# Backward of two normalisations: the mean and dot-product scalars scaled in place, and an affine part moved to ScalarE

## The chip, the cores and the metric

The kernel runs on one core of a Trainium2 chip. The metric is the device time of one launch in microseconds (us). A core has a matrix engine (TensorE, PE in the profile; its weight loads are PEld), a vector engine (VectorE, DVE), a scalar engine (ScalarE, ACT), a general engine (GpSimd, POOL) and an engine that issues transfers (SyncE, SP). Each works through its own list of instructions; an instruction can wait for one of another engine or for a transfer.

## The reference

The kernel computes the output and all gradients of a small two-layer model. A layer is a convolution part (A) and a feed-forward part (B), each on a normalised input and each added to its input:

```python
x = A_q
x = x + _A_ref(_layernorm(x, axis=-1), A_k, A_v, A_shift_k, A_ssm_k, A_ssm_D)
x = x + _B_ref(_layernorm(x, axis=-1), B_w1, B_w2)
x = x + _A_ref(_layernorm(x, axis=-1), A_k, A_v, A_shift_k, A_ssm_k, A_ssm_D)
x = x + _B_ref(_layernorm(x, axis=-1), B_w1, B_w2)
```

The sequence has 2048 rows of D = 448 features; B goes through F = 1792 hidden features with silu. A multiplies its normalised input n by a Y that is the same in both layers. For the backward pass of a normalisation with output n and incoming gradient u (already multiplied by 1/std), the gradient of its input is

    u - mean(u) - n * mean(u * n)

with both means over the 448 features, and the gradient that goes past the normalisation is added. This is what the change touches. It is computed 64 times, for 16 tiles of 128 rows, two layers and two normalisations in each.

## The kernel before

**Stages.** A prefix makes Y with a Fourier transform on TensorE (to about 110 us). Then come layer 1 forward, layer 2 forward woven with layer 2 backward (to about 395 us), layer 1 backward (to about 513 us), and a suffix with the weight gradients and the backward Fourier transform. The rows are worked in 4 chunks of 4 tiles (128 rows each). `L` is 1 for layer 2 and 0 for layer 1.

**One backward chunk.** `ga` multiplies the incoming gradient with w2 in seven pairs of 512-column products `ps_g`. Each pair lies in one of the two PSUM buffers of tag "mm". ScalarE copies it to `ghp` (L690), which frees the buffer for TensorE, and VectorE multiplies it with the silu slope into `ghT` (L698). The slopes are made in place by ScalarE (L614), in layer 1 from `dTl`, which is loaded back from HBM. Then `gn` runs for each of the four tiles: TensorE sums `ps_n` (14 products, L741), ScalarE moves it to `u0`, multiplied by 1/std, with its row sum as accumulator output into `cp` (L743), and `ln_bwd` on VectorE gives the gradient `g1` (in `X` for layer 2, in `G` for layer 1). VectorE makes `gYb` (L753, or L756 and L757) and `u1` with its row sum (L759), and a second `ln_bwd` follows for normalisation A. `u0` and `u1` share one tag with two buffers, so L743 of the next tile but one waits until VectorE is through with an earlier one.

**`ln_bwd`.** L716 multiplies u by n and accumulates the row sum into the second column of `cp`; L718 scales both columns by -1/448 into `cc`. In layer 2 and for the first normalisation of layer 1, two scalar_tensor_tensor follow (L727 adds n times the second scalar, L728 the first scalar and the residual). The second normalisation of layer 1 passes `s`: ScalarE then makes `v`, n times the second scalar plus the first (L721), and VectorE adds u, residual and v with two tensor_tensor (L722, L723).

**What else is in the queues.** In layer 2 the chunk's backward is woven with the next chunk's forward: `ps_h` products share the "mm" buffers, ScalarE makes `aT` (silu, L629) and VectorE `dT` (L113). After the last `aT` ScalarE loads a table and makes eight slopes before the next `na` (normalisation, L273) or `ghp`. In layer 1 products of a weight gradient (`ps_d`, L905) are put between the backward ones.

**Order.** A scheduler with costs for every instruction sets the order on each engine. A balancer (`k.bal`) that adds up estimated loads picks the engine of some copies and normalisations. Engines keep the order that the scheduler gave them.

Of the kernel before, what the change touches and what calls it, by code (L numbers as in the profile page):

```python
# [10 lines left out]
FP32 = mybir.dt.float32  # L11
BF16 = mybir.dt.bfloat16
ACT = mybir.ActivationFunctionType
ALU = mybir.AluOpType
# [3 lines left out]
P = 128  # L18
S = 2048
D = 448  # L20
# [227 lines left out]
def _pm(ap2d):  # L248
    return ap2d.rearrange("(p j) d -> p j d", j=J)
# [230 lines left out]
class Main:  # L480
# [231 lines left out]
    def ln_bwd(self, u0, n_t, cp, g_res, G_out, s=None):  # L712

        nc = self.nc
        junk = self.ch.tile([P, D], BF16, name="lb_junk", tag="lb_junk", bufs=1)
        nc.vector.scalar_tensor_tensor(out=junk[:], in0=u0, scalar=1.0, in1=n_t, op0=ALU.mult, op1=ALU.mult, accum_out=cp[:, 1:2])  # L716
        cc = self.ch.tile([P, 2], FP32, name="lb_cc", tag="lb_cc", bufs=2)
        nc.vector.tensor_scalar(out=cc[:], in0=cp, scalar1=-1.0 / D, scalar2=None, op0=ALU.mult)  # L718
        if s is not None:
            v = self.ch.tile([P, D], BF16, name="lb_v", tag="a_t1")  # L720
            nc.scalar.activation(v[:], n_t, ACT.Identity, bias=cc[:, 0:1], scale=cc[:, 1:2])  # L721
            nc.vector.tensor_tensor(out=s, in0=u0, in1=g_res, op=ALU.add)  # L722
            nc.vector.tensor_tensor(out=G_out, in0=s, in1=v[:], op=ALU.add)  # L723
            self.k.bal.add("dve", 1.5)
            self.k.bal.add("act", 0.64)
            return
        nc.vector.scalar_tensor_tensor(out=u0, in0=n_t, scalar=cc[:, 1:2], in1=u0, op0=ALU.mult, op1=ALU.add)  # L727
        nc.vector.scalar_tensor_tensor(out=G_out, in0=u0, scalar=cc[:, 0:1], in1=g_res, op0=ALU.add, op1=ALU.add)  # L728
        self.k.bal.add("dve", 2.0)

    def gn(self, c, L, ghT, nb, gres, na, hook=None):
        nc, k = self.nc, self.k
        sl = slice(4 * c, 4 * c + 4)
        si = 2 * L
        cp = self.ch.tile([P, 8, 2], FP32, name="cp", tag="cp", bufs=1)
        G = k.X[:, sl, :] if L == 1 else self.ch.tile([P, 4, D], BF16, name="G0", tag="gb", bufs=2)
        for tl in range(4):
            t = 4 * c + tl
            pn = k.psum.tile([P, 512], FP32, name="ps_n", tag="tr" if L == 1 and tl % 2 else "po", bufs=2)
            for ft in range(NF):  # L740
                mm = nc.tensor.matmul(pn[:, :D], lhsT=ghT[ft // 7][:, ft % 7, tl * P:(tl + 1) * P], rhs=self.w1T[:, ft, :], start=(ft == 0), stop=(ft == NF - 1))  # L741
            u0 = self.ch.tile([P, D], FP32, name="lb_u0", tag="lb_u0", bufs=2)
            last_u = nc.scalar.activation(u0[:], pn[:, :D], ACT.Identity, scale=k.rstd[2 * L + 1][:, t:t + 1], accum_out=cp[:, tl, 0:1])  # L743
            k.bal.add("act", 0.75)
            k.pe_engine = mm.ins.engine
            if L == 0:
                self.fill(2 if c < 3 else 12)
            if hook:
                hook(tl, mm.ins, last_u.ins)
            g1 = G[:, tl, :]  # L750
            self.ln_bwd(u0[:], nb[:, tl, :], cp[:, tl, :], gres(tl), g1)
            if L == 1:
                nc.vector.tensor_tensor(out=k.gYb[:, t, :], in0=g1, in1=na[:, tl, :], op=ALU.mult)  # L753
            else:
                gy = self.ch.tile([P, D], BF16, name="gy", tag="lb_junk", bufs=1)
                nc.vector.tensor_tensor(out=gy[:], in0=g1, in1=na[:, tl, :], op=ALU.mult)  # L756
                nc.vector.tensor_tensor(out=k.gYb[:, t, :], in0=gy[:], in1=k.gYb[:, t, :], op=ALU.add)  # L757
            u1 = self.ch.tile([P, D], BF16, name="lb_u1", tag="lb_u0", bufs=2)
            nc.vector.scalar_tensor_tensor(out=u1[:], in0=g1, scalar=k.rstd[si][:, t:t + 1], in1=self.Y[:, t, :], op0=ALU.mult, op1=ALU.mult, accum_out=cp[:, 4 + tl, 0:1])  # L759
            k.bal.add("dve", 1.2)  # L760
            self.ln_bwd(u1[:], na[:, tl, :], cp[:, 4 + tl, :], g1, g1, g1 if L == 0 else None)
        if L == 0:
            nc.gpsimd.dma_start(out=_pm(k.outs[1][0])[:, sl, :], in_=G[:])
        else:
            nc.gpsimd.tensor_copy(k.Xp[:, sl, D:], k.Xp[:, sl, 384:D])
# [458 lines left out]
```

## Time and profile before

| | us |
|---|---|
| median of 3 runs | 730.08 (729.82 to 730.56) |
| the profiled execution | 729.32 |
| its span | 727.5 |

| group, one instruction | count | mean ns |
|---|---|---|
| L716 dot product with accumulator, VectorE | 64 | 619 to 622 |
| L718 scaling of the two scalars, VectorE | 64 | 166 |
| L727 and L728 with `na`, layer 2, VectorE | 16 and 16 | 682 and 682 |
| L722 and L723, layer 1, VectorE | 16 and 16 | 385 and 388 |
| L721 `lb_v`, ScalarE | 16 | 759 |
| L743 `lb_u`, ScalarE | 32 | 632 |
| L690 `ghp`, ScalarE | 56 | 1005 |
| L614 slope of 128x1024, ScalarE | 48 | 1043 to 1050 |

From 258 to 395 us (layer 2 backward with forward) TensorE is busy for 132.22 of 137.00 us, VectorE for 108.80 and ScalarE for 94.66. From 395 to 516 us (layer 1 backward) it is 116.20, 105.29 and 75.03 of 121.00 us.

A line of a timeline gives start, duration, engine, line, operation, output and input, and in brackets the idle time before it and what ended it. A line of waits gives engine, line and what was waited for, then the total, the number and the longest.

### The profile page before, as it was taken

How to read it: one execution, taken by the hardware profiler on the slowest of the kernel's cores; microseconds unless marked ns; L12 is line 12 of the kernel's file. 1: busy time of each engine (PE TensorE's matmuls, PEld its weight loads, DVE VectorE, ACT ScalarE, POOL GpSimd, SP SyncE). 2: the span in 40 equal slices, each digit the busy share in tenths (PEclk: the TensorE clock that was granted, in tenths of full speed). 3: DMA queues.
4: the chain of work that ended last, by engine and by line, in shares of the span. 5: the costliest groups of instructions: out<-in, count | busy, mean ns of one | idle time of the engine just before them, and what ended most of it. 6: DMA issues, size and time to landing. Idle time of an engine off the chain costs nothing. (4 is left out here: it accounts for less than half of the span.)

```text
span 727.5 us, 12191 instructions
## 1 busy us (share of the span) xinstructions
PE 689.2 (95%) x4753; PEld 361.7 (50%) x4753; DVE 507.4 (70%) x1059; ACT 424.0 (58%) x539; POOL 55.0 (8%) x97
## 2 busy tenths in 40 slices
PE   5998889999999998999999899999999999999997
PEld 5676533444444443443444344444555667755553
DVE  4878978787743498795977998798223777179534
ACT  4788867767427757587485676762623666532101
POOL 1133021111100001000000000000000000000000
PEclk9999989999999999999999999999999999999999
DMA  9969959999976877878989999999699898999994
GB/s 301 244 205 253 371 202 315 246 315 292 250 155 145 189 189 169 217 186 211 236 207 310 239 316 257 243 302 288 229 270 226 271 349 334 309 269 238 239 217 99
DMA packets 234789, 180.11 MB, mean 248 GB/s; under 512 B 179178, under 2 KB 215598, under 8 KB 233580
## 3 DMA queue, kind: packets, MB, share of 16 engines
q1 hardware_dynamic: 230254, 163.68, 85.2%
q0 software_dynamic: 3856, 15.31, 6.7%
q8 instruction: 37, 0.61, 0.4%
q10 hardware_dynamic: 622, 0.35, 0.2%
q14 instruction: 20, 0.16, 0.1%
HBM read 69.58 MB, written 63.77 MB: 183 GB/s over the span
## 5 line engine op out<-in xcount | busy, mean ns | idle before, releaser
L905 PEld LDWEIGHTS <-dstat 128*128 128x128 bf16 x896 | 85.1, 98 | 77.5 <-issue 2.9
L537 PE MATMUL ps_h<-nT,w1sb 128*128 128x512 bf16 (+1 forms) x448 | 104.7, 389 | 6.6 <-DVE dT L113 5.1
L537 PE MATMUL ps_g<-gT,w2T 128*128 128x512 bf16 (+1 forms) x448 | 96.0, 381 | 3.4 <-ACT ghp L690 3.4
L741 PE MATMUL ps_n<-w1T,ghT 128*128 128x448 bf16 x448 | 90.2, 353 | 2.1 <-DVE ghT L698 2.0
L629 ACT ACTIVATE aT<-ps_h 128x1024 bf16<-128x1024 f32 (+1 forms) x64 | 58.4, 915 | 57.5 <-PE ps_h L537 40.5
L658 PE MATMUL ps_o<-w2sb,aT 128*128 128x448 bf16 x448 | 90.1, 353 | 0.0
L905 PE MATMUL ps_d<-mov,dstat 128*128 128x448 bf16 x448 | 89.2, 352 | 0.0
L113 DVE CAST dT<-ps_h 128x1024 bf16<-128x1024 f32 (+1 forms) x55 | 58.3, 1064 | 30.0 <-ACT aT L629 30.0
L537 PEld LDWEIGHTS <-w1sb 128*128 128x128 bf16 (+1 forms) x448 | 36.4, 97 | 71.5 <-issue 43.6
L537 PEld LDWEIGHTS <-w2T 128*128 128x128 bf16 (+1 forms) x448 | 35.4, 96 | 62.3 <-issue 29.7
L741 PEld LDWEIGHTS <-ghT 128*128 128x128 bf16 x448 | 42.8, 98 | 44.2 <-DVE ghT L698 4.3
L690 ACT CAST ghp<-ps_g 128x1024 bf16<-128x1024 f32 x56 | 55.3, 1005 | 14.9 <-PE ps_g L537 10.3
L658 PEld LDWEIGHTS <-aT 128*128 128x128 bf16 x448 | 42.4, 98 | 42.4 <-issue 3.8
L905 PE MATMUL ps_d<-X,dstat 128*128 128x448 bf16 x224 | 52.1, 353 | 0.0
L905 PE MATMUL ps_d<-GO,dstat 128*128 128x448 bf16 x224 | 50.3, 353 | 0.8 <-DMA dstat<-A_d 0.8
L743 ACT ACTIVATE lb_u<-ps_n,rstd 128x448 f32<-128x448 f32 x32 | 20.2, 632 | 39.1 <-DVE X L728 17.7
L227 PEld LDWEIGHTS <-pa 128*128 128x128 bf16 x336 | 32.8, 98 | 7.1 <-DVE pa L451 4.2
L228 PEld LDWEIGHTS <-pb 128*128 128x128 bf16 x336 | 32.5, 98 | 7.5 <-DVE pb L452 4.0
L967 ACT CAST dout<-ps_d 128x448 bf16<-128x448 f32 x14 | 7.5, 534 | 48.8 <-PE ps_d L905 48.8
L698 DVE TENSOR_TENSOR ghT<-dT,ghp 128x1024 bf16<-128x1024 bf16 (+1 forms) x32 | 19.7, 621 | 20.5 <-ACT ghp L690 20.3
L614 ACT ACTIVATE dTl<-dTl 128x1024 bf16<-128x1024 bf16 (+1 forms) x32 | 29.8, 943 | 6.6 <-DMA dTl<-DT_d 6.6
L659 DVE TENSOR_TENSOR X<-X,ps_o 128x448 bf16<-128x448 bf16 x32 | 19.7, 616 | 16.3 <-PE ps_o L658 16.2
(186 smaller groups left out, 1083.2 us busy)
## 6 DMA issues: line engine op xcount, KB each, us to landing
A_d<-turned SPq DMA_DIRECT2D x12, 896.0 KB, 4.6
GH_d<-turned SPq DMA_DIRECT2D x12, 896.0 KB, 4.8
dstat<-A_d SPq DMA_DIRECT2D x21, 512.0 KB, 4.9
dstat<-GH_d SPq DMA_DIRECT2D x21, 512.0 KB, 4.8
DT_d<-dT SPq DMA_DIRECT2D x8, 896.0 KB, 6.4
dTl<-DT_d SPq DMA_DIRECT2D x8, 896.0 KB, 6.8
spec_K<-Z SPq DMA_DIRECT2D x7, 512.0 KB, 17.1
KB<-Z POOLq DMA_DIRECT2D x14, 256.0 KB, 12.0
```

What stands on the lines that cost most here:

```text
L113: eng.tensor_copy(out, in_)
L227: nc.tensor.matmul(o, lhsT=pa[:, i * P:(i + 1) * P], rhs=k.Gsb[:, ga, :], start=True, stop=False)
L228: nc.tensor.matmul(o, lhsT=pb[:, i * P:(i + 1) * P], rhs=k.Gsb[:, gb, :], start=False, stop=True)
L537: self.nc.tensor.matmul(o, lhsT=w[lo:hi, b, f:f + P], rhs=r, start=(seen[u] == 1), stop=(seen[u] == ND))
L614: self.k.last_slope = self.nc.scalar.activation(s, s, ACT.Derivative_silu)
L629: last = nc.scalar.activation(a, ps[:, 0:n, :], ACT.Silu)
L658: nc.tensor.matmul(po[:, :D], lhsT=aT[ft // 7][0][:, ft % 7, tl * P:(tl + 1) * P], rhs=self.w2sb[:, ft, :], start=(ft == 0), stop=(ft == N ...
L659: nc.vector.tensor_tensor(out=X[:, t, :], in0=X[:, t, :], in1=po[:, :D], op=ALU.add)
L690: k.last_gh = nc.scalar.copy(gh[:], ps[:])
L741: mm = nc.tensor.matmul(pn[:, :D], lhsT=ghT[ft // 7][:, ft % 7, tl * P:(tl + 1) * P], rhs=self.w1T[:, ft, :], start=(ft == 0), stop=(ft == ...
L743: last_u = nc.scalar.activation(u0[:], pn[:, :D], ACT.Identity, scale=k.rstd[2 * L + 1][:, t:t + 1], accum_out=cp[:, tl, 0:1])
L905: i = k.nc.tensor.matmul(ps[:, :D], lhsT=st[:, t, :], rhs=mov[:, t, :], start=start and t == 0, stop=stop and t == NT - 1)
```

## The change

The sum's scalar does the scaling in two places at once: the product u times n is multiplied by -1/448 inside L716's instruction, whose accumulator output then goes straight into the second column of `cc`; and the first column is made from the row sum by an ACTIVATE with Identity on ScalarE. The scaling on VectorE is gone, `cp` keeps one column for each sum, and `cc` has three buffers. In layer 2 the second normalisation now passes `s` too, so that it takes the branch with `v` on ScalarE and two tensor_tensor. The instruction's lines in the changed kernel are L717 (ScalarE) and L718 (VectorE's product).

```diff
         junk = self.ch.tile([P, D], BF16, name="lb_junk", tag="lb_junk", bufs=1)
-        nc.vector.scalar_tensor_tensor(out=junk[:], in0=u0, scalar=1.0, in1=n_t, op0=ALU.mult, op1=ALU.mult, accum_out=cp[:, 1:2])
-        cc = self.ch.tile([P, 2], FP32, name="lb_cc", tag="lb_cc", bufs=2)
-        nc.vector.tensor_scalar(out=cc[:], in0=cp, scalar1=-1.0 / D, scalar2=None, op0=ALU.mult)
+        cc = self.ch.tile([P, 2], FP32, name="lb_cc", tag="lb_cc", bufs=3)
+        nc.scalar.activation(cc[:, 0:1], cp, ACT.Identity, scale=-1.0 / D)
+        nc.vector.scalar_tensor_tensor(out=junk[:], in0=u0, scalar=-1.0 / D, in1=n_t, op0=ALU.mult, op1=ALU.mult, accum_out=cc[:, 1:2])
         if s is not None:
             v = self.ch.tile([P, D], BF16, name="lb_v", tag="a_t1")
             nc.scalar.activation(v[:], n_t, ACT.Identity, bias=cc[:, 0:1], scale=cc[:, 1:2])
...
-        cp = self.ch.tile([P, 8, 2], FP32, name="cp", tag="cp", bufs=1)
+        cp = self.ch.tile([P, 8], FP32, name="cp", tag="cp", bufs=1)
...
-            last_u = nc.scalar.activation(u0[:], pn[:, :D], ACT.Identity, scale=k.rstd[2 * L + 1][:, t:t + 1], accum_out=cp[:, tl, 0:1])
+            last_u = nc.scalar.activation(u0[:], pn[:, :D], ACT.Identity, scale=k.rstd[2 * L + 1][:, t:t + 1], accum_out=cp[:, tl:tl + 1])
...
-            self.ln_bwd(u0[:], nb[:, tl, :], cp[:, tl, :], gres(tl), g1)
+            self.ln_bwd(u0[:], nb[:, tl, :], cp[:, tl:tl + 1], gres(tl), g1)
...
-            nc.vector.scalar_tensor_tensor(out=u1[:], in0=g1, scalar=k.rstd[si][:, t:t + 1], in1=self.Y[:, t, :], op0=ALU.mult, op1=ALU.mult, accum_out=cp[:, 4 + tl, 0:1])
+            nc.vector.scalar_tensor_tensor(out=u1[:], in0=g1, scalar=k.rstd[si][:, t:t + 1], in1=self.Y[:, t, :], op0=ALU.mult, op1=ALU.mult, accum_out=cp[:, 4 + tl:5 + tl])
             k.bal.add("dve", 1.2)
-            self.ln_bwd(u1[:], na[:, tl, :], cp[:, 4 + tl, :], g1, g1, g1 if L == 0 else None)
+            self.ln_bwd(u1[:], na[:, tl, :], cp[:, 4 + tl:5 + tl], g1, g1, g1)
```

## The prediction

> **What bounds the kernel now.** I read the page's busy table first, then TensorE's own waits over the whole span, then the order-of-time views of the two backward stretches (258 to 395 us for layer 2, 395 to 516 us for layer 1).
>
> ```profile
> PE 689.2 (95%) x4753; PEld 361.7 (50%) x4753; DVE 507.4 (70%) x1059; ACT 424.0 (58%) x539; POOL 55.0 (8%) x97
> ```
>
> TensorE is the bound: its work is fixed by the change, so only its 727.5 - 689.2 = 38.3 us of idle time can move. From 516 us on the windows show it busy to the end (206.93 of 211.5 us, and 4.3 of the 4.6 us idle lie after 720 us), so what the backward stretches lose or gain there arrives whole at the end. The chain of waits runs through VectorE at 498 to 514 us, but beside it TensorE does dW matmuls (ps_d), so that chain is worth only the gap it makes. The waits of TensorE from 300 to 530 us are:
>
> ```profile
> PE ps_g L537 <- ACT ghp L690: 2.3, 5, 0.9
> PE ps_n L741 <- DVE ghT L698: 2.0, 3, 0.7
> PE ps_t L548 <- ACT nb L273: 1.1, 3, 0.4
> PE ps_d L905 <- DMA dstat<-A_d: 0.8, 1, 0.8
> PE ps_s L205 <- ACT A1g L111: 0.3, 1, 0.3
> ```
>
> With 258 to 300 us (0.6 us for dT on VectorE, 1.1 us each for ghp and nb on ScalarE) the stretch holds only some 9.2 us of gaps. VectorE's backlog makes about 4.2 of them (dT 0.6, ghT 2.0, and the ghp waits at 404, 430 and 458 us, 1.6, where ScalarE stood behind VectorE): that is all a lighter VectorE can win. Everything turns on ghp: ScalarE's copy of ps_g frees one of the two PSUM buffers "mm", without which TensorE stops. ScalarE's timeline of one chunk shows what shares its queue with these copies:
>
> ```profile
> 447.73 0.63 ACT L743 ACTIVATE lb_u<-ps_n,rstd 128x448 f32<-128x448 f32 x1 [1.11 <-DVE G L728]
> 448.26 0.19 ACT L743 ACTIVATION_READ_ACCUMULATOR lb_u<-ps_n,rstd 128x1 f32 x1
> 448.36 1.04 ACT L614 ACTIVATE dTl<-dTl 128x1024 bf16<-128x1024 bf16 x1
> 450.12 0.76 ACT L721 ACTIVATE lb_v<-na_l,lb_cc 128x448 bf16<-128x448 bf16 x1 [0.72 <-DVE lb_cc L718]
> 450.90 1.01 ACT L690 CAST ghp<-ps_g 128x1024 bf16<-128x1024 f32 x1
> 452.42 0.63 ACT L743 ACTIVATE lb_u<-ps_n,rstd 128x448 f32<-128x448 f32 x1 [0.51 <-DVE G L728]
> ```
>
> and before it, in the same chunk:
>
> ```profile
> 443.35 1.06 ACT L614 ACTIVATE dTl<-dTl 128x1024 bf16<-128x1024 bf16 x1 [2.81 <-DMA dTl<-DT_d]
> ```
>
> The reader is to see that ScalarE is 58% busy but already waits in line: for the dTl load (6.6 us in three waits, at 391.29, 443.35 and 468.52 us), for VectorE's sums, for buffers.
>
> **What the Trainium skill says.** "PSUM — Partial Sum Buffer", section "Engine vs sequencer instructions": the queues of ScalarE and VectorE are strict FIFO. The trace agrees: at 443.35 us the next L743 stands 2.8 us behind the waiting L614, though VectorE had freed its buffer. "VectorE: DVE Perf Modes", the perf-mode tier table: a tensor_tensor on bf16 runs in the 2x mode. Here it takes 385 ns (L722), against 682 ns for scalar_tensor_tensor on the same size (L727, L728).
>
> **The change, part by part.**
>
> *VectorE.* 64 L718 of 166 ns go: 10.6 us, 0.33 per tile. In layer 2, 16 times two of 682 ns become two of 387 ns: 16 x 0.59 = 9.4 us. Together 20.0 us off 507.4, 3.7 us per layer-2 chunk and 1.3 us per layer-1 chunk. The sums' own L716 is as before with another scalar. That cp loses a column and lb_cc gets a third buffer costs nothing: no wait for either is among TensorE's. The balancer's other bookings change no choice: the built program has the same normalisations and PSUM copies on ScalarE.
>
> *ScalarE.* Added: 64 scalings of 128x1 and 16 affine parts. The trace has no such scaling; nearest are the 128x4 ACTIVATE (206 ns) and the read of the accumulator (195 ns). "ScalarE: Activation LUTs", "What ACT_TABLE_LOAD costs", gives 186 ns for immediate scale and bias, 93 less back to back: bounds 0.10 and 0.21, I take 0.17. 64 x 0.17 = 11 us. The affine part is L721, 760 ns busy and 0.68 back to back: 16 x 0.68 = 11 us. The same page ("Table sets") puts Identity into every set; the built program has as many table loads as before. So ScalarE goes to some 447 us; as a sum that is hidden. Its place in the queue isn't.
>
> *Order.* Built, the changed program keeps the matmuls' order but for shifts of a few. On SP, loads of gb and nb_l step ahead of one A_d store and a dstat load past a GP_d store; nothing waits for these, I price them at 0 (if they collide, up to 0.5 either way). On ScalarE the new instructions fall at bad places, and I follow each.
>
> *(a) End of each layer-2 chunk.* Between the last aT and the first ghp ScalarE runs table load and slopes without a hole; the order puts a scaling and a lb_v among the eight slopes: 0.17 + 0.68 = 0.85. At 364 to 375.75 us (third chunk) that is all on the path (TensorE waits 0.33 us for ghp there): +0.85. At 276.81 and 324.95 us na (L273) waited 0.65 and 0.61 us for VectorE's L727, which no longer reads na: +0.25 each. Sum +1.35.
>
> *(b) dT in layer 2.* After 20 ps_h TensorE needs aT and dT of the two mm buffers. The order has lb_v of the second tile ahead of the 512-wide aT. In the first chunk, taking VectorE's spacings (0.60 independent, 0.72 dependent), that aT comes at 260.7 instead of 259.89, its dT ends at 262.4 instead of 261.5: gaps of 0.65 and 0.35 against 0.25 and 0.35, so +0.4. In the second and third there is no ps_o left between the ps_h: +0.25 each. Sum +0.9.
>
> *(c) 387 to 413 us.* The order on ScalarE is L743, slope of dTl, then the first scaling. The slope waits for its load until 391.29, so the scaling ends at 392.45 and VectorE's L728, which ran at 390.18, waits for it: a stall of 2.3 us, some 1.7 when (a) has moved TensorE but not the load. Behind it all of VectorE's tile chain shifts, and ghp's second copy now stands behind the next L743, a slope and the scaling that waits for L759. Followed through, TensorE has the third ps_g pair some 1.6 late and the fourth 3.0; the gaps of 0.54, 0.60 and 0.66 us are taken back. Net +1.6.
>
> *(d) 413 to 439 us.* No load waits. ghp stays in place, the second is 1 us later, but VectorE is 1.3 us lighter and the 0.72 us gap at 439.23 goes: -0.5.
>
> *(e) 440 to 465 us.* The clearest place. L743 at 439.82; slope until 444.3; scaling until 444.46; L728 at 444.5 instead of 442.17. VectorE's L759 of the third tile then ends at 455.05. The order puts L743 of tile four, a 0.5 us slope, the scaling after that L759 and one more ahead of the first ghp: 455.6 to 456.55 instead of 450.90. TensorE needed it at 453.09: 3.5 late. The 0.91 us gap at 457.99 goes in it, and 0.2 more: net +2.4.
>
> *(f) 466 to 491 us.* The same order; the load's wait was 1.08 and shrinks to some 0.45, as TensorE comes later. ghp starts at about 480.2 (from 477.80), needed by 479.99: ends 1.2 late. +1.2 (bounds 0.8 and 1.9).
>
> *(g) 498 to 516 us.* VectorE's chain is 4 x 0.36 = 1.4 us shorter, the 0.29 gap goes, the 0.76 us wait for dstat (its load is ahead of a store now) shrinks: -0.8.
>
> Sum: 1.35 + 0.9 + 1.6 - 0.5 + 2.4 + 1.2 - 0.8 = 6.15 us. On the profiled execution, 729.32 (span 727.5 and 1.8 around it), that is 735.5; the median of the runs is 0.76 above it: 736.2.
>
> **Rivals.**
> 1. *VectorE's relief decides (faster).* For it: VectorE is 9.8 to 10.0 of 10 us busy from 400, 420 and 450 us on, and 4.2 us of gaps hang on it. If the loads land before the slopes need them, (c), (e), (f) lose their stall and ghp comes as VectorE frees it. Then 2.3 us of (a) and (b) stand against 4.2 of gaps and 0.8 of (g): -2.7, 727.4. Against it: even without the stall ghp stands behind a scaling that waits for VectorE.
> 2. *The two cancel (no change).* The scaling is short, ghp has a slack of about 1 us (453.09 against 451.9), and the shifted load absorbs most of the stall: (c), (e), (f) make +0.8 each, (a) and (b) half, 1.1, (d) and (g) -1.3, and 1.9 us of VectorE's gaps are won besides: +0.3, 730.4.
> 3. *Worse than forecast.* The lateness in (c), (e), (f) isn't regained and SP's transposes, at DMA shares above 1.0 there, push the loads back as well: 3.0 + 3.4 + 1.9 + 2.3 = +10.6, 740.7.
>
> Rival 1 is the other side's mechanism: it decides once the three load waits are below about 0.5 us.
>
> **How the numbers follow.** Forecast 0.60 (732 to 739), rival 1 0.17, rival 2 0.13, rival 3 0.10. A measurement here tells about 0.2% (1.5 us) from no change. Faster 0.17; same 0.12; slower 0.71. Leaving out the far halves of rivals 1 and 3, the range is 728 to 740; the forecast's own is 732 to 739.
>
> **What would show it.** L718's small form gone, 64 of 128x1 on ScalarE near 0.2 us; DVE near 487 and ACT near 447 us busy. TensorE's waits for ghp up from 3.4 (whole span) to about 8 to 11 us, the longest near 3 us around 455 to 460; ghT and dT waits down. VectorE waiting for the scaling at L728, at two or three places of 0.6 to 2.3 us behind a slope that waits for dTl. Wrong would be: ghp waits no larger than before, or L728 not waiting; then rival 1 or 2 holds. Gaps that grow at ps_d or after 516 us would mean a cause in the DMA that I don't price.

## The result and the profile after

The changed kernel takes 734.53 us (median of 8 runs, 732.68 to 737.99) against 729.95 us (8 runs, 728.23 to 731.51) for the kernel before: a ratio of 1.0074, 95% interval 1.0047 to 1.0101. It is 4.6 us slower; an estimated 0.8 us of that goes with a lower granted clock in the changed kernel's runs (last section). The profiled execution took 735.11 us, with a span of 733.3 against 727.5.

The busy table of the page, in the changed kernel:

```profile
PE 688.8 (94%) x4753; PEld 362.7 (49%) x4753; DVE 491.9 (67%) x995; ACT 442.2 (60%) x619; POOL 54.9 (7%) x97
```

VectorE (DVE) is 15.5 us lighter, ScalarE (ACT) 18.2 us busier, TensorE's work is what it was. So the 5.8 us by which the span grew are idle time of TensorE (44.5 us against 38.3). Its waits from 300 to 530 us (us in total, times, longest):

```profile
PE ps_g L537 <- ACT ghp L690: 10.8, 7, 3.9
PE ps_t L548 <- ACT nb L273: 1.1, 3, 0.4
PE ps_s L205 <- ACT A1g L111: 0.7, 1, 0.7
PE ps_n L741 <- DVE ghT L698: 0.3, 1, 0.3
```

The waits for VectorE's ghT fell from 2.0 to 0.3 us: VectorE's relief did arrive. The waits for ScalarE's copy of PSUM, ghp, grew from 2.3 to 10.8 us. TensorE's timeline shows where (only the lines with larger gaps are printed, the others are left out at the dots); the bracket at a line's end is the idle time ahead of it and who ended it:

```profile
376.55 8.25 PE L537 MATMUL ps_g<-gT,w2T 128*128 128x512 bf16 x40 [1.08 <-ACT ghp L690]
...
402.62 2.73 PE L537 MATMUL ps_g<-gT,w2T 128*128 128x512 bf16 x8 [3.90 <-ACT ghp L690]
...
432.56 1.79 PE L537 MATMUL ps_g<-gT,w2T 64*128 64x512 bf16 x8 [1.10 <-ACT ghp L690]
...
459.27 1.78 PE L537 MATMUL ps_g<-gT,w2T 128*128 128x512 bf16 x8 [2.84 <-ACT ghp L690]
...
486.40 1.78 PE L537 MATMUL ps_g<-gT,w2T 128*128 128x512 bf16 x8 [1.28 <-ACT ghp L690]
```

There is one gap of more than 1 us in each layer-1 chunk, in the places where the kernel before had 0.54, 0.18, 0.91 and none. The chunk at 440 to 465 us shows the mechanism best. On ScalarE:

```profile
445.85 1.06 ACT L614 ACTIVATE dTl<-dTl 128x1024 bf16<-128x1024 bf16 x1 [2.12 <-DMA dTl<-DT_d]
446.81 0.19 ACT L717 ACTIVATE lb_cc<-cp 128x1 f32<-128x1 f32 x1
...
456.89 0.63 ACT L743 ACTIVATE lb_u<-ps_n,rstd 128x448 f32<-128x448 f32 x1 [1.60 <-DVE G L728]
457.43 0.19 ACT L743 ACTIVATION_READ_ACCUMULATOR lb_u<-ps_n,rstd 128x1 f32 x1
457.52 0.62 ACT L614 ACTIVATE dTl<-dTl 128x512 bf16<-128x512 bf16 x1
458.04 0.28 ACT L717 ACTIVATE lb_cc<-cp 128x1 f32<-128x1 f32 x2
458.22 1.00 ACT L690 CAST ghp<-ps_g 128x1024 bf16<-128x1024 f32 x1
```

and VectorE in the same chunk:

```profile
444.43 0.69 DVE L727 SCALAR_TENSOR_TENSOR lb_u<-nb_l,lb_cc,lb_u 128x448 f32<-128x448 bf16 x1
447.03 0.69 DVE L728 SCALAR_TENSOR_TENSOR G<-lb_u,lb_cc,X 128x448 bf16<-128x448 f32 x1 [1.92 <-ACT lb_cc L717]
```

The reader is to see three steps. The slope (L614) waits 2.12 us for its load; the scaling of 0.19 us stands behind it though its input was ready at 443.7; VectorE, which has done L727, waits 1.92 us for one column. From then on VectorE's chain of tiles is late, ScalarE's next evictions (L743) wait for it, and the first ghp, which the kernel before had ahead of the fourth eviction, at 450.90 us, starts at 458.22 behind it.

The last step also works by itself. In the chunk at 466 to 491 us no slope waits for a load and VectorE doesn't wait for a scaling, and still TensorE stands for 1.28 us. ScalarE there:

```profile
472.31 1.04 ACT L614 ACTIVATE dTl<-dTl 128x1024 bf16<-128x1024 bf16 x1
...
484.02 0.63 ACT L743 ACTIVATE lb_u<-ps_n,rstd 128x448 f32<-128x448 f32 x1 [1.60 <-DVE G L728]
...
484.64 0.62 ACT L614 ACTIVATE dTl<-dTl 128x512 bf16<-128x512 bf16 x1
485.16 0.28 ACT L717 ACTIVATE lb_cc<-cp 128x1 f32<-128x1 f32 x2
485.35 1.00 ACT L690 CAST ghp<-ps_g 128x1024 bf16<-128x1024 f32 x1
```

The first ghp stands behind the fourth eviction, a slope and two scalings; in the kernel before it ran ahead of that eviction (477.80 against 479.28 us).

### The profile page after: what moved, and what is told of

It reads as the page before. It is cut to its first block, busy times and chain, and to the rows that moved or that the text cites. A ratio compares the mean times of both kernels' runs of the same rounds, so it can differ in the third digit from the quotient of the medians.

```text
span 733.3 us, 12271 instructions
## 1 busy us (share of the span) xinstructions
PE 688.8 (94%) x4753; PEld 362.7 (49%) x4753; DVE 491.9 (67%) x995; ACT 442.2 (60%) x619; POOL 54.9 (7%) x97
## 4 chain that ended last, share of the span: by engine, by line
PE 48%; DVE 20%; ACT 11%; DMA 10%; issue 6%; SPq 2%; POOL 2%; ACTq 0%; DVEq 0%; POOLq 0%
PE ps_d L905 20%; PE ps_o L658 7%; PE ps_h L537 5%; PE ps_g L537 4%; DMA spec_K<-Z 3%; DVE dT L113 3%; DVE lb_junk L718 3%; DMA dTl<-DT_d 2%; DVE lb_u L727 2%; PE ps_v L227 2%; DVE lb_u L759 2%; PE ps_v L228 2%; PE ps_s L205 2%; DMA K_sb<-in_A_ssm_k_dram 2%; DMA spec_KV<-A1K 1%
## 5 line engine op out<-in xcount | busy, mean ns | idle before, releaser
L537 PE MATMUL ps_g<-gT,w2T 128*128 128x512 bf16 (+1 forms) x448 | 97.6, 385 | 11.6 <-ACT ghp L690 11.6
L537 PE MATMUL ps_h<-nT,w1sb 128*128 128x512 bf16 (+1 forms) x448 | 101.7, 381 | 7.0 <-DVE dT L113 5.3
L690 ACT CAST ghp<-ps_g 128x1024 bf16<-128x1024 f32 x56 | 55.6, 1006 | 14.4 <-PE ps_g L537 10.8
L743 ACT ACTIVATE lb_u<-ps_n,rstd 128x448 f32<-128x448 f32 x32 | 20.2, 632 | 31.2 <-DVE X L728 11.5
L614 ACT ACTIVATE dTl<-dTl 128x1024 bf16<-128x1024 bf16 (+1 forms) x32 | 30.0, 945 | 7.1 <-DMA dTl<-DT_d 7.1
```

Of the source, the lines that this page charges most:

```text
L537: self.nc.tensor.matmul(o, lhsT=w[lo:hi, b, f:f + P], rhs=r, start=(seen[u] == 1), stop=(seen[u] == ND))
L614: self.k.last_slope = self.nc.scalar.activation(s, s, ACT.Derivative_silu)
L690: k.last_gh = nc.scalar.copy(gh[:], ps[:])
```

## The experiments

The theory (queue theory below) is that the loss comes from the place of the first normalisation's scaling in ScalarE's queue. The rivals are the amount of work added to ScalarE, at whatever place, and the order of the DMAs on SyncE, which the change moved too. Times are medians of 22 runs (14 for e4_scale_first and e8_pool_sums, 15 for e12_load_order, 6 for e11_second_only); each ratio is to the kernel before in runs on the same chip in turn, with its 95% interval in brackets.

**The sums alone and the affine part alone.** e1_sums_only is the changed kernel with

```
-            self.ln_bwd(u1[:], na[:, tl, :], cp[:, 4 + tl:5 + tl], g1, g1, g1)
+            self.ln_bwd(u1[:], na[:, tl, :], cp[:, 4 + tl:5 + tl], g1, g1, g1 if L == 0 else None)
```

> The changed kernel, with layer 2's second normalisation back on VectorE alone; the two new ways of making the sums stay in both layers. If ScalarE's queue order carries the loss (the scaling stands behind a slope that waits for its load, and PSUM copies stand behind scalings that wait for VectorE), the places in layer 1 stay as in the changed kernel: the longest gap of TensorE at 388 to 413 us about 3.9, the gaps at 440 to 465 about 2.8 and at 466 to 491 about 1.3 us, VectorE's one wait of 4 to 5 us for the scaling stays, and the time is 732.5 to 734.5. If it is the amount of work on ScalarE, most of that amount (16 x 0.76 us) is gone here and the time is 730 to 731.5.

e2_affine_only is the kernel before with the opposite edit, in L761.

> The kernel before, with only layer 2's second normalisation moved to ScalarE; both sums are scaled by VectorE as before. If the queue order of the scaling carries the loss: 729 to 731, the gaps of TensorE in layer 1 within 0.5 us of before's (1.8, 0.9, 0.9, 0). If the amount of work on ScalarE carries it: 732.5 to 734, with copies of PSUM late wherever layer 2's affine part stands ahead of them.

Measured: the sums alone 732.44 us, 1.0043 [1.0026, 1.0060]; the affine part alone 730.90, 1.0022 [1.0005, 1.0038]. 3.0 and 1.4 us come near the 4.6. In e1_sums_only the gaps at 458 and 485 us are there (3.33 and 1.02 us), but from 388 to 416 us they are 1.8 in all where the changed kernel has 4.5, and VectorE's wait for the scaling there is 0.5 us, not the 4 to 5 expected: ScalarE waited only 0.7 us for that load. Both times agree with the queue theory's numbers (732.44 lies at their lower edge); that the affine part costs anything isn't explained by it. Gaps grew at the ends of the layer-2 chunks. TensorE in e2_affine_only:

```profile
280.79 8.25 PE L537 MATMUL ps_g<-gT,w2T 128*128 128x512 bf16 x40 [1.35 <-ACT ghp L690]
...
329.38 8.25 PE L537 MATMUL ps_g<-gT,w2T 128*128 128x512 bf16 x40 [0.56 <-ACT ghp L690]
...
378.73 8.24 PE L537 MATMUL ps_g<-gT,w2T 128*128 128x512 bf16 x40 [1.31 <-ACT ghp L690]
```

against 1.09, 0.29 and 0.33 before: 1.51 us more. But the gaps at 413 to 440 and 440 to 465 us, in layer 1, grew too, from 0.90 to 1.35 and from 0.91 to 1.82 us, and in the second of these places ScalarE waited 4.0 us for dTl, where it had waited 2.8 before.

**The same work in another order.** e4_scale_first makes the first scaling directly behind the eviction, and ties the slopes to it instead of to the eviction; `ln_bwd` takes this `cc` and makes no scaling of its own (the eviction's line is shortened at the dots):

```
             last_u = nc.scalar.activation(u0[:], pn[:, :D], ...)
+            cc = self.ch.tile([P, 2], FP32, name="lb_cc", tag="lb_cc", bufs=3)
+            last_u = nc.scalar.activation(cc[:, 0:1], cp[:, tl:tl + 1], ACT.Identity, scale=-1.0 / D)
```

> The changed kernel with the same operations on the same engines; only the first normalisation's scaling is put directly behind the eviction that makes its sum, ahead of the slopes and what else is ordered behind that eviction. If the order carries the loss through VectorE's wait for a scaling behind a slope: VectorE's waits for the scaling at 4.5 and 1.9 us are gone, the gap of TensorE at 388 to 413 falls from 3.9 to 1.5 to 2.5, those at 440 to 465 from 2.8 to about 1, and the time is 730.5 to 732.5. The second normalisation's scalings, which wait for VectorE, stay, so it is not back at 730. If the amount of ScalarE work carries it, this changes nothing: 734 to 735.

Measured: 730.75 us, 1.0009 [0.9989, 1.0029]. With every operation on the same engine as in the changed kernel, most of the 0.74% is gone. TensorE's gaps in e4_scale_first:

```profile
401.19 5.13 PE L537 MATMUL ps_g<-gT,w2T 128*128 128x512 bf16 x16 [2.49 <-ACT ghp L690]
...
431.27 1.79 PE L537 MATMUL ps_g<-gT,w2T 64*128 64x512 bf16 x8 [1.01 <-ACT ghp L690]
...
455.76 1.78 PE L537 MATMUL ps_g<-gT,w2T 128*128 128x512 bf16 x8 [0.61 <-ACT ghp L690]
458.02 1.79 PE L537 MATMUL ps_g<-gT,w2T 64*128 64x512 bf16 x8 [0.19 <-ACT ghp L690]
482.22 1.78 PE L537 MATMUL ps_g<-gT,w2T 128*128 128x512 bf16 x8 [0.32 <-ACT ghp L690]
484.48 1.79 PE L537 MATMUL ps_g<-gT,w2T 64*128 64x512 bf16 x8 [0.19 <-ACT ghp L690]
```

VectorE has no wait for the scaling any more, and 3.90, 2.84 and 1.28 us became 2.49, 0.80 and 0.51. Amount alone can't be the cause. Nor can SyncE's order: it is the same as in the changed kernel (the store of A_d is issued at 379.17 us in both), and ScalarE still waits 4.24 and 1.72 us for dTl. The edit moved one thing more than was meant: in the chunks at 440 to 465 and 466 to 491 us the first ghp now directly follows the fourth eviction (at 454.71 and 481.17 us), ahead of the slope and the scalings that stood before it for 0.7 us. That is part of what it won there.

**The scaling off ScalarE.** e3_scale_dve is the changed kernel with

```
-        nc.scalar.activation(cc[:, 0:1], cp, ACT.Identity, scale=-1.0 / D)
+        nc.vector.tensor_scalar(out=cc[:, 0:1], in0=cp, scalar1=-1.0 / D, scalar2=None, op0=ALU.mult)
```

> The changed kernel, with the scaling of the one column made by VectorE in place of ScalarE; all else as changed, the affine part of layer 2 on ScalarE too. If the scaling's place in ScalarE's queue carries the loss: the loss is gone and 728 to 730.5 is left, TensorE's waits for the PSUM copy back to 3 to 5 us in all, VectorE without a wait for the scaled column. If the amount of ScalarE work carries it: only 64 x 0.2 us of it is taken away, about half of the added amount, so about 732; VectorE, which has more to do, is later by up to 64 x 0.1 us and the time may stay at 734.

Measured: 729.61 us, 1.0002 [0.9985, 1.0019]: in the time the loss is gone, as the queue theory has it. The trace doesn't show it: TensorE's waits for ghp are 8.4 us, not 3 to 5, and ScalarE waits 12.3 us for dTl, once 6.0. The profiled execution isn't typical. It took 731.05 us, where the four others with the same granted clock (1.000) took 726.26 to 727.43, although its first 225 us, untouched by the edit, were 2.9 us shorter than in the kernel before. So this run's time counts for the theory, its trace doesn't.

**First scaling or second.** In e11_second_only only the second scaling is on VectorE, the first stays where the changed kernel has it; e5_second_dve does the same to e4_scale_first. The edit of e11_second_only:

```
+        if g_res is G_out:
+            nc.vector.tensor_scalar(out=cc[:, 0:1], in0=cp, scalar1=-1.0 / D, scalar2=None, op0=ALU.mult)
+        else:
             nc.scalar.activation(cc[:, 0:1], cp, ACT.Identity, scale=-1.0 / D)
```

> The changed kernel with the second normalisation's scaling on VectorE; the first one's stays on ScalarE where the order puts it, behind the slopes. If the first scaling behind the waiting slope is the loss by itself: the loss stays, VectorE's waits for the scaling at L728 stay at 1.9 to 4.5 us, TensorE's gap at 388 to 413 stays above 3 and the one at 440 to 465 above 2, the time is 733 to 735. If the second scaling, which waits for VectorE with the PSUM copies behind it, is as large a part: about half is taken back, 731 to 732.5.

> As e4_scale_first (first scaling directly behind the eviction, on ScalarE), and the second normalisation's scaling made by VectorE, so that ScalarE no longer waits for VectorE's product ahead of the PSUM copies. If the queue order is the whole loss and the second scaling is what is left of it: TensorE's gaps at 388 to 413 and at 413 to 440 fall from 2.5 and 1.0 to within 0.5 us of the kernel before (1.8 and 0.9 in all there), and the time is 1 us or more below e4_scale_first, 728 to 730. If what is left in e4_scale_first is the affine part of layer 2 on ScalarE (its run alone cost 1.6 us): no change against e4_scale_first, 730 to 731.5.

Measured: e11_second_only 735.52 us, 1.0076 [1.0047, 1.0105]; e5_second_dve 730.66, 1.0017 [0.9998, 1.0036]. The loss stays whole with the second scaling off ScalarE, and the rest that e4_scale_first leaves doesn't shrink. VectorE's waits in e11_second_only from 380 to 520 us (L731 is L728 there, L720 is L717):

```profile
DVE X L731 <- ACT lb_cc L720: 3.9, 1, 3.9
...
DVE G L731 <- ACT lb_cc L720: 2.1, 2, 1.6
```

Its largest gaps of TensorE are 3.40 and 2.60 us in the old places. So of the two scalings it is the first, behind the slope that waits, that carries the loss.

**Without layer 2's affine part.** e6_first_sums is e4_scale_first, e7_dve_sums is e3_scale_dve, each with the edit of e1_sums_only; e8_pool_sums is e7_dve_sums with the column scaled by GpSimd.

> As e4_scale_first, with layer 2's second normalisation back on VectorE. If the parts add as they did so far (4.6 us for the whole, 3.0 for the sums, 1.6 for the affine part), this is 1.6 below e4_scale_first: 728.5 to 730, at or just below the kernel before. If VectorE's relief by the affine part is what lets e4_scale_first recover: above it, 731 to 733.

> The kernel before with one edit of the sums alone: VectorE scales one column and the product by its scalar; ScalarE does nothing new. VectorE does the same number of operations as before (the scaling of 128x2 becomes one of 128x1), but the scaling no longer stands between the product and the add. If the affine part costs 1.6 us here too, this is 1.6 below e3_scale_dve: 727 to 729. If it is only ScalarE's place for the scaling that was bad and all else is neutral: 729 to 730.5, as before.

> As e7_dve_sums, with the one column scaled by GpSimd, which is busy 8% of the span. If the loss of the change is the queue in which the scaling waits, an engine with a short queue hides it, and VectorE is 64 operations lighter: 727 to 729, VectorE's busy time about 497. If a GpSimd operation takes 1 us or more with its signals, each tile's chain on VectorE is longer by that and the time is 730 to 734.

Measured, in this order: 729.14 us, 0.9987 [0.9974, 1.0001]; 728.56 us, 0.9985 [0.9969, 1.0000]; 730.36 us, 1.0015 [0.9991, 1.0040]. Against their partners e4_scale_first and e3_scale_dve the ratios of the first two are 0.22 and 0.17 percentage points lower, about what the affine part cost alone; by itself neither difference is clear of the intervals. e7_dve_sums is the best of all, 0.9 points below the changed kernel; whether it beats the kernel before, by 0.15%, its interval doesn't settle (the last section does). GpSimd met neither expectation: its operation takes 378 ns, not a microsecond, and yet the time lies among those expected for a microsecond.

**Where the affine part costs.** e9_affine_three is e2_affine_only, e10_dve_three is e7_dve_sums, both with `g1 if L == 0 or tl < 3 else None`.

> As e2_affine_only, with the affine part on ScalarE for the first three tiles of each layer-2 chunk and the fourth back on VectorE. In the second and third chunk no such part then stands among the slopes ahead of the first PSUM copy. If that place carries the affine part's loss of 1.5 us (TensorE's gaps at the end of the three chunks were 1.35, 0.56 and 1.31 against 1.09, 0.29 and 0.33): the second and third gap are 0.4 or less, the first stays at 1 to 1.4, and the time is 729.3 to 730.3. If the amount on ScalarE carries it: three quarters of the loss stay, 730.5 to 731, with the gaps spread.

> As e7_dve_sums, with the affine part on ScalarE for the first three tiles of each layer-2 chunk: the relief of VectorE without the instruction among the slopes. If relief of VectorE in layer 2 is worth anything to TensorE, 0.3 to 0.8 us below e7_dve_sums: 727.5 to 728.5. If TensorE doesn't wait for VectorE there: as e7_dve_sums, 728.5 to 729.2.

Measured: e9_affine_three 731.18 us, 1.0014 [0.9996, 1.0033], with 0.56, no and 1.04 us at the three chunks' ends; e10_dve_three 730.63 us, 1.0028 [1.0004, 1.0051]. Neither expectation of either run came true as written. ScalarE's order shows that e9_affine_three didn't quite test the place: in the second and third chunk the third tile's part stands ahead of an aT, and the chain aT, slopes, first ghp runs without a hole, so it can delay that as well. e10_dve_three says that VectorE's relief in layer 2 doesn't pay for the work on ScalarE: with both the time is 0.43 points higher than without. Its trace has the loss in layer 1, which the edit doesn't touch: ScalarE waits 11.4 us for dTl (e7_dve_sums: 5.3), and TensorE from 300 to 530 us 8.1 us for ghp (3.3). That the affine part costs time by making these loads land later is a guess that no run tested.

**The order on SyncE.** e12_load_order swaps one pair of the changed kernel on SyncE and nothing else:

```
-                nl = self.load_n(0)
+                with self.tc.issue_after(self.stores[-2].ins): nl = self.load_n(0)
```

(`stores` keeps what `flush` issues; this one is the store of A_d.)

> The changed kernel with one pair swapped on SyncE, and every other engine's order the same: the load of nb_l stands behind the store of A_d again, as in the kernel before. If that move, which the prediction priced at nothing, is why the load of dTl landed late (SyncE issued the store at 379.17 in place of 377.64, and with it the transposes and the load 1.5 us later): the store is back at about 377.6, ScalarE's wait for dTl near 391 falls from 4.7 to about 3, TensorE's gap at 388 to 413 from 3.9 to 2.2 to 2.8, and the time is 732.5 to 733.8. If the load is late for another reason: the gap stays at 3.5 or more and the time at 734 to 735.5.

Measured: 734.88 us, 1.0073 [1.0049, 1.0097]. SyncE in the changed kernel (start, us in the queue):

```profile
374.95 0.82 SPq L777 DMA_DIRECT2D nb_l<-N_d  x1
379.17 0.36 SPq L504 DMA_DIRECT2D A_d<-turned  x1
...
383.98 2.98 SPq L503 DMA_TRANSPOSE turned<-ghT  x1
387.02 0.56 SPq L770 DMA_DIRECT2D dTl<-DT_d  x1
```

and in e12_load_order:

```profile
377.75 0.37 SPq L504 DMA_DIRECT2D A_d<-turned  x1
378.36 0.36 SPq L777 DMA_DIRECT2D nb_l<-N_d  x1
...
382.66 2.86 SPq L503 DMA_TRANSPOSE turned<-ghT  x1
385.57 0.72 SPq L770 DMA_DIRECT2D dTl<-DT_d  x1
```

The load is issued 1.45 us earlier, ScalarE's wait for it falls from 4.69 to 2.37 us, VectorE's wait at L728 from 4.5 to 2.2, and TensorE's gaps at 388 to 416 us from 4.47 to 3.26 in all. In the trace that is the first expectation, but for the gaps, which are split in two; in the time, 734.88, it is the second. The interval, 1.8 us either way, can hide the 1.2 us. So one trace shows an earlier load, and the time shows no gain. The order by itself doesn't make the store late either: e1_sums_only and e7_dve_sums have the load of nb_l ahead of it too and issue the store 2.0 and 2.2 us after that load, where the changed kernel takes 4.2. With e4_scale_first above, SyncE's order is ruled out as the cause of the loss.

## Why the prediction was right

It forecast a loss of 6.15 us, and with it 736.2 us; the medians differ by 4.6, and the time is 734.53. The gaps of TensorE in the two profiles give, place by place:

| step | forecast | measured | gaps before, after |
|---|---|---|---|
| (a) ends of layer-2 chunks | +1.35 | +0.53 | 1.09, 0.29, 0.33; 0.84, 0.32, 1.08 |
| (b) dT in layer 2 | +0.9 | +0.15 | 0.25, 0.35; 0.54, 0.21 |
| (c) 387 to 413 us | +1.6 | +2.67 | 0.54, 0.60, 0.66; 3.90, 0.25, 0.32 |
| (d) 413 to 440 us | -0.5 | +0.20 | 0.18, 0.72; 1.10 |
| (e) 440 to 465 us | +2.4 | +1.93 | 0.91; 2.84 |
| (f) 466 to 491 us | +1.2 | +1.28 | none; 1.28 |
| (g) 498 to 522 us | -0.8 | -0.36 | 0.76, 0.29; 0.69 |

These make 6.40. The span grew by 5.8: the part ahead of 227 us, which the change doesn't touch, was 1.1 us shorter in this execution, and TensorE was busy 0.5 us longer in the stretch (248.91 us against 248.42). That 6.40 comes so near to 6.15 is partly luck: the terms miss by up to 1.1 us each, and the misses cancel.

The mechanism of (c) and (e) held step for step: a slope waits for its load, the scaling stands behind it, VectorE waits for the scaling, and ghp comes late. e4_scale_first shows it by taking it away, e11_second_only by keeping it without the second scaling. It agrees with what the Trainium skill's "PSUM — Partial Sum Buffer", section "Engine vs sequencer instructions", states, that ScalarE's queue is a strict FIFO: the scaling with its input ready at 443.7 us ran at 446.81, behind the slope. In its own example of this the prediction read too much: the next L743, said to stand 2.8 us behind the slope, had its product complete only at 442.81 us and ran at 444.31, so it lost 1.5 at most.

These terms were off:
- (a) and (b), forecast at 2.25, measured 0.68. The third chunk's 0.85 came (0.75), but the first two chunks' ends were 0.25 better and 0.03 worse, not 0.25 worse each; and in the second and third chunk TensorE had no wait for dT at all.
- (c), short by 1.07. Here failed, as far as two traces show, the step on SyncE that the prediction priced at nothing: with "On SP, loads of gb and nb_l step ahead of one A_d store" went a load of dTl that was issued 1.5 us later, where the prediction let the wait shrink. With the pair swapped back the gaps of (c) are 1.46 above the kernel before, close to the 1.6 forecast.
- (d) had the wrong sign: the ghp at 431.51 us stands behind a scaling that waited 0.31 and a lb_v that waited 0.49 us for VectorE.
- (f) has the right size with half the mechanism. The wait for a load that was to remain, some 0.45 us, is not there, and L728 follows L727 without a wait; the 1.28 us come with the place of ghp behind the fourth eviction (which waits 1.60 us for VectorE), the slope and two scalings.
- (g): the wait of 0.76 us for dstat went, but the gap of 0.29 us, which was to go, grew to 0.69.

The scaling took 196 ns in the mean where 170 was taken, inside the bounds. ScalarE's total, 442.2 where 447 was forecast, and VectorE's, 491.9 where 487 was, are no terms of the sum. The durations of VectorE's instructions did fall by the 20.0 us forecast; the busy time fell by 15.5, because neighbours overlap and the overlap counts once (in the kernel before a scaling at 471.97 us lasts 0.17, and the next instruction starts at 472.05).

Rival 1 fails in the changed kernel, since two load waits stayed above 2 us, well over the 0.5 us it needed. Its claim that VectorE's relief would then win isn't borne out either: with the scaling off ScalarE, e3_scale_dve only comes back to the kernel before, and the affine part, which is about half of the relief (9.4 of 20.0 us), cost 1 to 3 us in every pair (e2_affine_only against the kernel before, the changed kernel against e1_sums_only, e4_scale_first against e6_first_sums, e3_scale_dve and e10_dve_three against e7_dve_sums). Where these microseconds are lost stays open: e2_affine_only's gaps point to the chunk ends and to layer 1, e10_dve_three's to layer 1, and e9_affine_three neither confirms nor excludes the chunk ends.

## What to carry to other kernels

Work moved to an engine with room is priced by the instruction that it lands behind, not by its duration: look for instructions in the new queue that wait for a DMA, and put what another engine needs at once ahead of them, here directly behind the operation that makes its input. Look as well for what the new instructions push back: here the copy that frees a PSUM buffer came to stand behind an eviction, a slope and two scalings. When one engine's order changes, read the DMA queue's order too: here a load of 448 KB came ahead of a store, and in the trace another load was issued 1.5 us later for it, though in the time nothing of this could be seen. And take relief of an engine that TensorE hardly waits for as worth nothing until a trace shows it.

## What the runs showed of the hardware

One and the same scaling of 128x1 took 196 ns on ScalarE, 148 on VectorE and 378 on GpSimd. The groups of L717, in the changed kernel, in e7_dve_sums and in e8_pool_sums (count, busy us, mean ns, idle time ahead and who ended it):

```profile
L717 ACT ACTIVATE lb_cc<-cp 128x1 f32<-128x1 f32 x64 | 11.1, 196 | 14.3 <-DVE lb_u L759 14.1
```

```profile
L717 DVE TENSOR_SCALAR lb_cc<-cp 128x1 f32<-128x1 f32 x64 | 9.5, 148 | 9.3 <-ACT lb_u L743 9.0
```

```profile
L717 POOL TENSOR_SCALAR lb_cc<-cp 128x1 f32<-128x1 f32 x64 | 23.6, 378 | 196.8 <-DVE lb_u L759 129.0 <-ACT lb_u L743 67.7 <-POOL lb_cc L717 0.2
```

Two of them back to back on ScalarE took 0.28 us (458.04 us above), so that a second costs less than 0.1 more; the duration was never the problem.

Single executions spread more than the effects here, and most of the spread goes with the granted clock, the share of TensorE's full clock that an execution was given in the mean. In 196 runs of the kernel before, beside the experiments on four chips, the times go from 725.61 to 734.98 us:

| granted clock | runs | median us |
|---|---|---|
| 0.989 to 0.992 | 15 | 733.70 |
| 0.993 to 0.994 | 52 | 730.90 |
| 0.995 to 0.996 | 71 | 729.60 |
| 0.997 to 0.998 | 38 | 728.60 |
| 0.999 to 1.000 | 20 | 727.72 |

A straight line through these runs falls by 7.0 us for 0.01 of clock. The changed kernel's eight runs had a clock of 0.9934 in the mean against 0.9956 for these; whether the change itself lowers the clock isn't shown. With the line taken out, the means differ from the kernel before by these estimates (95% interval in brackets):

| run | us | run | us |
|---|---|---|---|
| changed kernel | +3.7 [3.2, 4.3] | e12_load_order | +3.8 [3.0, 4.5] |
| e1_sums_only | +2.2 [1.7, 2.7] | e2_affine_only | +2.0 [1.5, 2.6] |
| e4_scale_first | +0.5 [-0.1, 1.2] | e6_first_sums | -1.3 [-1.8, -0.9] |
| e3_scale_dve | +1.2 [0.3, 2.1] | e7_dve_sums | -1.2 [-1.9, -0.4] |
| e11_second_only | +3.4 [2.4, 4.3] | e10_dve_three | +0.9 [0.3, 1.5] |
| e5_second_dve | +1.6 [1.1, 2.2] | e8_pool_sums | +0.7 [0.2, 1.4] |
| e9_affine_three | +1.4 [0.8, 2.1] | | |

They part the change more clearly than the medians do. The sums alone, with the scaling on VectorE or directly behind the eviction, gain 1.2 to 1.3 us; the first scaling's place behind the slope, with what it does to ghp, costs 3.2 to 3.5 (the changed kernel against e4_scale_first, e1_sums_only against e6_first_sums); the affine part costs 1.5 to 2.4. What e3_scale_dve and e4_scale_first keep is, about, the affine part's cost less the sums' gain. And e12_load_order doesn't differ from the changed kernel, to within 1 us.

The clock isn't all: the start of the first ps_g run on TensorE, before anything that the experiments touch, lay between 225.3 and 228.6 us in the profiles.
